# Four half tiles of K as a second seven-product unit, in a new order of the program, on one core

## The chip, the cores and the metric

The kernel runs on one core of one Trainium2 chip. The metric is the time of one execution in microseconds of device time. The runs of the kernel before gave a median of 203.47 us (three runs, 203.33 to 203.54).

## The reference

One input x of 2048 tokens by 640, normalized per token, feeds a linear attention (A) and a two-layer network with relu (B); the output joins them.

```python
def _A_ref(x, wqkv, wo):
    H = 32; Dh = D // H                      # D = 640
    q, k, v = ...                            # x @ wqkv, by heads
    phi = lambda t: jnp.where(t > 0, t + 1, jnp.exp(t)) + 1e-6
    pq, pk = phi(q), phi(k)
    kv = jnp.einsum("bhsd,bhse->bhde", pk, v)
    z = jnp.einsum("bhsd->bhd", pk)
    num = jnp.einsum("bhqd,bhde->bhqe", pq, kv)
    den = jnp.einsum("bhqd,bhd->bhq", pq, z)[..., None] + 1e-6
    return (num / den, heads joined) @ wo

def _B_ref(x, w1, w2):                       # w1: 640 x 1728, w2: 1728 x 640
    return jnp.maximum(x @ w1, 0) @ w2

xn = _layernorm(x)
return x + _A_ref(xn, wqkv, wo) * silu(_B_ref(xn, w1, w2))
```

All arrays are bf16.

## The kernel before

The 2048 tokens are 16 tiles of 128, in four chunks of 512. The kernel records its operations in a list and has two ways of ordering them. For TensorE (PE) and for SyncE (SP, which issues most DMAs) the order is that of `PROGRAM`, a string of some 500 words written out. For ScalarE (ACT), VectorE (DVE) and GpSimd (POOL) a planner, `Sched.place`, picks from the next 60 recorded operations by their costs (`cost`, an occupation and a duration in us for each form of instruction) and by due times counted back from PE's end. Both orders are fixed when the program is built; on the chip only semaphores hold an engine.

A head, not part of `PROGRAM`, loads x and weights, takes the statistics of the tiles, and computes K for tiles 0 to 7 (`K_mm`, L713) and the first blocks of h = xn @ w1 on the first chunk (`H_block`, L803). Then the words of `PROGRAM` follow:

- `n8` to `n15`: statistics (`bn`, L634; `aggr`, L638) and normalization (`LN_norm`, L653) of a tile, then its transpose by DMA on SP (`xnT_dma`, L702). `xa`, `xb`, `xc` load tiles 10 and 11, 12 and 13, 14 and 15; `wa` and `wb` load parts of w1.
- Units of seven products for eight. Four block products over two token blocks (or chunks) are formed with Strassen's sums: a unit has the steps s1, s5, s6, s2, s7, s3, s4, each a few matmuls into one of three PSUM banks, with two ScalarE copies (s1's and s5's results, L1209) and two VectorE additions (in s6 and s7) besides the evacuations. `a`, `b` are units of h over the first and second pair of chunks (512 columns), `p`, `q` those of Q, `m` a mixed one, `g` units of the product G = xn^T pk, `u` and `o` those of the second layer and of the output. They stand at L1202 (a, b, p, q, m, k) and L1029 (g, u, o).
- `k1` is a unit of K: tiles 9 and 13 (tile index 1 in the third and fourth chunk), with 320 columns a matmul. The sums of wk that it reads are made by `SK` (`k_S`). Its evacuations are exps and relus at L1331.
- `Ka8`, `Kb8` and so on compute one half (320 columns) of K for one tile by five matmuls, with an exp and a relu out of PSUM (`K_half`, L1486). Tiles 8, 10, 11, 12, 14 and 15 are done so. `K_fin` (L739) joins exp and relu to pk.
- `hh0` and `hh1` compute the last 64 columns of h for a pair of chunks (`H_half`, L821): twenty matmuls of 32 columns of weights, four of which stand side by side in the array (`tile_position`). Two ScalarE relus of 64 partitions each evacuate them (L827). `hh0` needs the transposed tiles 0 to 7, `hh1` tiles 8 to 15. `T1` forms sums of the transposed tiles for the `b`, `q` and `k` units.
- `y0` to `y15`, `zm`, `zs`, `zc`: POOL adds the tiles of pk into two sums by chained DMAs (L901); the column sum z comes of it. `dn` takes the denominators (L933) and four reciprocals (L946); `do0` to `do3` store them repeated into DRAM (L953), `rc0` to `rc3` read them back (L962), `dv` multiplies Q by them.
- `wv0`, `wv1` load w_v on ACT's queue (L544); `kv0`, `kv1` multiply G by it (L1599), `W0` to `W5` by wo (L1625), with small stores into the joined weight (L1640). `uT1` to `uT4` are sums of w2, `oT` sums of the joined weight.
- `e`, `f`, `l`: the last tiles of the output (L1834 and after).

The places of the units' rooms matter for `wv0`: g units copy a product into a part of wv_sb, so `wv0` waits until the g units have read it.

The change touches the words `Ka10`, `Kb10`, `Ka14`, `Kb14`, which become the unit `k2` (tiles 10 and 14), the places of `hh0` and `hh1` and of most other words, and the cost of an ACT operation. The whole unit is written already; its number is the tile index in the chunk:

```python
return unit(1, lambda half, k: wk[:, k, HN * half:HN * (half + 1)], ...,
            {1: ("kS", 1), 2: ("kS", 2), 4: ("kS", 4), 3: ("kS3",)}, out, out22, tile=i)
```

Of the kernel before, what the change touches and what calls it, by code (L numbers as in the profile page):

```python
# [32 lines left out]
def _cols(ap):  # L33
    n = 1
    for d in ap.shape[1:]:
        n *= d
    return n


def _wide(ap):  # L40
    return str(ap.dtype).endswith("float32")


def cost(E, fn):
    seen = _Seen()
    fn(seen)
    name, a, k = seen.call
    aps = [v for v in list(a) + list(k.values()) if hasattr(v, "shape") and hasattr(v, "dtype")]
    if E == "PE":
        if name == "transpose":  # L50
            return (0.107, 0.107) if a[1].offset % a[1].ap[0][0] < 640 else (0.056, 0.107)
        n = _cols(k["rhs"]) / 2400.0
        part = k["lhsT"].shape[-1] / 128.0 if k.get("tile_position") is not None else 1.0
        return max(n * part + 0.0025, 0.026), n
    n = max(_cols(v) for v in aps)
    if E == "ACT":
        more = 0.19 if k.get("accum_out") is not None else 0.0
        if n > 512:
            more += 0.02
        if n == 1 and k["func"] == ACTF.Silu:  # L60
            more += 1.3
        if hasattr(k.get("scale"), "shape"):
            more += 0.08
        if _wide(k["out"]) and _wide(k["in_"]) and k["out"].tensor.name == k["in_"].tensor.name:
            return 0.05 + 0.0009 * n, 0.17 + 0.00083 * n
        return 0.05 + 0.00083 * n + more, 0.17 + 0.00083 * n + more
    if E == "POOL":
        return (0.66, 0.66) if k.get("op") is ALU.pow else (0.33 + 0.0025 * n, 0.33 + 0.0025 * n) if n > 12 else (0.33, 0.33)
    out = k["out"] if "out" in k else a[0]
    wide = any(_wide(v) for v in aps if _cols(v) > 4)  # L70
    if name == "bn_stats":
        return 0.403, 0.478
    if n <= 12:
        return 0.13, 0.21
    if name == "reciprocal":
        return 0.815, 0.9
    if name in ("tensor_copy", "tensor_scalar", "memset"):
        more = 0.06 * sum(hasattr(k.get(q), "shape") for q in ("scalar1", "scalar2"))
        return (0.065 + 0.00105 * n, 0.15 + 0.00105 * n) if wide else (0.08 + 0.00024 * n + more, 0.16 + 0.00025 * n + more)
    if wide or name != "tensor_tensor":  # L80
        return 0.064 + 0.00105 * n, 0.155 + 0.00105 * n
    return 0.075 + 0.000515 * n, 0.148 + 0.00052 * n
# [12 lines left out]
class Sched:  # L95
# [44 lines left out]
    def _record(self, E, kind, fns, R, W, extra, sem=None):  # L140
# [5 lines left out]
        if kind == "dma":  # L146
            seen = _Seen()
            fns[0](seen)
            name, a, _k = seen.call
            o.turn = "transpose" in name  # L150
            o.occ = 1.3 if o.turn else 1.25 if E == "POOL" else 0.5
            fat = a[1].tensor.name
            if fat in ("in_A_wo_dram", "reg3") and E == "SP" and not o.turn:
                o.occ = 0.65
            size = 2.0
            for d in a[0].shape:
                size *= d
            names = [v.tensor.name for v in a[0:2]]
            o.byt = 0.6 if o.turn else size / {"scr": 205e3}.get(names[0], {"scr": 240e3}.get(names[1], 310e3))
            lag = 0.5 if names[1] == "scr" else 0.8 if names[1] == "reg3" and names[0] == "reg6" else 0.0  # L160
            if o.turn and names[0] == "wv_sb":
                o.byt = 2.0
            o.dur = 4.6 if E == "POOL" else 2.1 + o.byt if o.turn else 1.95 + o.byt + lag
        else:
            o.occ, o.dur = 0.0, 0.0
            o.turn = E == "PE" and any(_narrow(fn) for fn in fns)
            for fn in fns:
                occ, dur = cost(E, fn)
                o.dur = o.occ + dur
                o.occ += occ  # L170
# [1789 lines left out]
```

## Time and profile before

| | |
|---|---|
| median of three runs | 203.47 us (203.33 to 203.54) |
| the profiled execution's own time | 202.95 us |
| its span in the trace | 201.7 us |
| busy: PE, DVE, ACT, POOL | 198.4, 172.9, 129.1, 37.9 us |

The span is the time from the first to the last instruction of the profiled execution; the time around it is start and end of the launch. A busy PE is not PE at its peak: matmuls are pipelined and the trace models their ends, so lengths of work on PE are read from start to start, as the chain of waits does. In the page, PEld is the loading of weights, which runs beside PE. L12 is line 12 of the kernel before; in the changed kernel all lines behind the cost function are one higher.

### The profile page before, as it was taken

The numbers are of one execution on the slowest core, as the hardware profiler recorded it, in microseconds if no ns is written. First come the engines' busy times: TensorE is split into PE (matmuls) and PEld (weight loads), VectorE is DVE, ScalarE is ACT, GpSimd is POOL, SyncE is SP. The second block draws the span as 40 slices with busy tenths as digits, with TensorE's granted clock in tenths as the row PEclk, the third lists the DMA queues.
The fourth block names the chain that finished last, engine by engine and source line by source line (L and its number), as shares of the span: only waits on it lengthen the run. The fifth ranks groups of instructions, "written<-read, shape, count | busy, mean of one in ns | idle before, by whom it ended". The sixth has DMA issues, their size and how long they took to land.

```text
span 201.7 us, 3704 instructions
## 1 busy us (share of the span) xinstructions
PE 198.4 (98%) x1342; PEld 122.7 (61%) x1342; DVE 172.9 (86%) x411; ACT 129.1 (64%) x271; POOL 37.9 (19%) x66
## 2 busy tenths in 40 slices
PE   8999999999999999999999999999999999999995
PEld 7756544454554444445555677777767777777773
DVE  4998999999999987899975799789979799953566
ACT  5697969899889869998643213544445455452552
POOL 3183151253335550262200000000000000000000
DMA  6986992635556977365930988486983361020103
GB/s 204 330 218 112 268 237 48 165 95 118 126 117 137 183 154 183 65 132 88 240 65 0 313 246 194 150 216 182 368 293 79 128 184 68 26 81 28 65 33 98
DMA packets 38472, 30.43 MB, mean 151 GB/s; under 512 B 13750, under 2 KB 38454, under 8 KB 38454
## 3 DMA queue, kind: packets, MB, share of 16 engines
q1 hardware_dynamic: 32581, 23.28, 40.9%
q0 software_dynamic: 4624, 5.57, 14.4%
q10 hardware_dynamic: 1248, 1.35, 2.0%
q8 instruction: 10, 0.16, 0.4%
q14 instruction: 9, 0.07, 0.1%
HBM read 15.81 MB, written 5.24 MB: 104 GB/s over the span
## 4 chain that ended last, share of the span: by engine, by line
PE 96%; DMA 1%; DVE 1%; issue 0%; DVEq 0%
PE psT L1029 42%; PE psT L1202 30%; PE psT L713 9%; PE psT L803 5%; PE psT L1500 2%; DMA reg<-in_A_x_dram 1%; PE psT L1834 1%; PE psT L821 1%; PE psT L765 1%; PE psT L1625 1%; PE psT L686 1%; PE psT L1599 1%; PE psT L933 1%; DVE reg L974 0%; DVE stats L634 0%; DVE reg L679 0%
## 5 line engine op out<-in xcount | busy, mean ns | idle before, releaser
L1202 PE MATMUL psT<-reg 128*128 128x512 bf16 (+2 forms) x150 | 39.8, 374 | 0.0
L1029 PE MATMUL psT<-reg,regH 128*128 128x320 bf16 (+1 forms) x224 | 35.0, 299 | 0.0
L1029 PE MATMUL psT<-reg 128*128 128x320 bf16 (+1 forms) x178 | 29.2, 299 | 0.0
L1029 PEld LDWEIGHTS psT<-reg,regH 128*128 128x128 bf16 (+1 forms) x224 | 21.8, 98 | 8.6
L1202 PEld LDWEIGHTS psT<-reg 128*128 128x128 bf16 (+1 forms) x150 | 14.3, 98 | 16.8 <-DVE regH L974 0.8
L901 POOL DMA_DIRECT2D regH<-reg x16 | 18.4, 1210 | 30.1 <-DMA regH<-reg 11.7
L1036 ACT ACTIVATE reg<-psT 128x320 f32<-128x320 f32 (+1 forms) x24 | 10.4, 436 | 18.0 <-PE psT L1029 16.0
L1029 PEld LDWEIGHTS psT<-reg 128*128 128x128 f16 (+1 forms) x178 | 17.3, 98 | 7.4 <-issue 0.4
L974 DVE TENSOR_TENSOR reg<-reg 128x1024 f16<-128x1024 bf16 (+10 forms) x30 | 19.0, 649 | 0.1
L1661 ACT ACTIVATE wv_sb<-psT 128x320 bf16<-128x320 f32 (+1 forms) x23 | 9.6, 423 | 14.0 <-PE psT L1029 13.7
L1252 ACT ACTIVATE regH<-psT 128x512 bf16<-128x512 f32 (+1 forms) x24 | 15.0, 631 | 4.1 <-PE psT L1202 3.9
L974 DVE TENSOR_TENSOR psT<-psT,reg 128x320 f32<-128x320 f32 (+1 forms) x21 | 11.4, 545 | 5.4 <-PE psT L1029 5.1
L713 PE MATMUL psT<-reg 128*128 128x320 bf16 x100 | 15.5, 299 | 0.0
L1029 PE MATMUL psT<-reg,pqT 128*128 128x320 bf16 (+1 forms) x84 | 15.3, 299 | 0.0
L634 DVE BATCH_NORM_STATS2 stats<-reg 128x6 f32<-128x320 bf16 x32 | 14.0, 474 | 1.3 <-DMA reg<-in_A_x_dram 1.3
L974 DVE TENSOR_TENSOR reg<-psT,reg 128x320 bf16<-128x320 f32 (+2 forms) x17 | 8.5, 502 | 5.9 <-PE psT L1029 5.9
L713 PEld LDWEIGHTS psT<-reg 128*128 128x128 bf16 x100 | 9.8, 98 | 5.6
L1036 ACT ACTIVATE psT<-psT 128x320 f32<-128x320 f32 x17 | 7.0, 423 | 7.4 <-PE psT L1029 7.4
L780 ACT ACTIVATE regE<-psT 128x512 bf16<-128x512 f32 x16 | 9.9, 617 | 2.9 <-PE psT L1202 1.9
L1486 ACT ACTIVATE regE<-psT 128x320 bf16<-128x320 f32 x24 | 10.5, 514 | 0.6 <-PE psT L713 0.6
L1849 ACT ACTIVATE reg<-psT 128x640 bf16<-128x640 f32 (+1 forms) x14 | 7.4, 569 | 4.5 <-PE psT L1029 4.5
L642 POOL TENSOR_TENSOR rsy<-rsv,mhalf 128x1 f32<-128x1 f32 x16 | 10.1, 635 | 1.1
(169 smaller groups left out, 395.6 us busy)
## 6 DMA issues: line engine op xcount, KB each, us to landing
regH<-reg POOLq DMA_DIRECT2D x16, 320.0 KB, 3.7
reg<-in_B_w_dram SPq DMA_DIRECT2D x12, 320.0 KB, 5.0
scr<-rden SPq DMA_DIRECT2D x4, 640.0 KB, 6.2
reg<-in_A_x_dram SPq DMA_DIRECT2D x4, 640.0 KB, 8.0
out_dram<-reg SPq DMA_DIRECT2D x14, 160.0 KB, 1.9
regE<-scr SPq DMA_DIRECT2D x3, 640.0 KB, 4.9
reg<-in_A_x_dram SPq DMA_DIRECT2D x4, 320.0 KB, 3.5
reg<-in_A_wo_dram SPq DMA_DIRECT2D x6, 160.0 KB, 5.0
```

The lines of the kernel that those rows point to most:

```text
L634: sc.op("DVE", lambda eng: eng.bn_stats(stats[:, t, a, :], xv[:, HN * a:HN * (a + 1)]), R=[("xin", xs(t))], W=[("stats", t, a)])
L642: sc.op("POOL", lambda eng: eng.tensor_tensor(out=rsy[:, t:t + 1], in0=rsv[:, t:t + 1], in1=mhalf[:, :], op=ALU.pow), R=[("rsv", t), ("mha ...
L713: fns.append(lambda eng, a=a, k=k, lhs=lhs: eng.matmul(ps[bk[a]][:, 0:HN], lhsT=lhs, rhs=wk[:, k, HN * a:HN * (a + 1)], start=(k == 0), st ...
L780: exps.append(sc.op("ACT", lambda eng: eng.activation(out=e_, in_=src, func=ACTF.Exp), R=[key], W=[("er_e", es)]))
L803: sc.group("PE", [(lambda eng, k=k: eng.matmul(ps[b], lhsT=w1_col(k, P * f, P), rhs=src[:, k, :], start=(k == 0), stop=(k == C - 1))) for ...
L901: dma("POOL", lambda eng: eng.dma_start(zacc[a], src, **kw), R=[key] + after, W=[("zacc", a)], chain=zchain[a])
L974: sc.op("DVE", lambda eng: eng.tensor_tensor(out=out, in0=in0, in1=in1, op=op), R=R, W=W, extra=extra)
L1029: sc.group("PE", [(lambda eng, k=k, lhs=lhs, rhs=rhs: eng.matmul(ps[b][:, 0:HN], lhsT=lhs, rhs=rhs, start=(start and k == 0), stop=(k == n ...
L1036: sc.op("ACT", lambda eng: eng.activation(out=dst, in_=ps[b][:, 0:HN], func=ACTF.Copy), R=[("ps", b)], W=[dkey], extra=extra)
L1202: sc.group("PE", [(lambda eng, k=k, lhs=lhs, rhs=rhs: eng.matmul(ps[b][:, 0:nn], lhsT=lhs if tile is None else rhs, rhs=rhs if tile is Non ...
L1252: sc.op("ACT", lambda eng: eng.activation(out=dst, in_=ps[b], func=ACTF.Relu), R=[("ps", b)], W=[("hT", j, f)], extra=ex)
L1486: sc.op("ACT", lambda eng, func=func, slot=slot: eng.activation(out=ek[:, eks(t), slot, HN * a:HN * (a + 1)], in_=ps[b][:, 0:HN], func=fun ...
```

## The change

1. The four groups `Ka10`, `Kb10`, `Ka14` and `Kb14` of `K_half` are taken out, and the unit `k2` stands in `PROGRAM`.
2. `hh0` and `hh1` stand one behind the other; before, `hh0` came early and `hh1` 34 us later. Most other words have other places, too: among PE's words the units and K halves are mixed in another way, and on SP `xb` and `xc` come behind tile 8's transpose, tiles 9 to 15 are transposed in one run, `rc0` and `rc1` come earlier, `do3` comes before `do1`, and the stores of the W words come behind `rc1`.
3. In the planner's costs an ACT operation whose output has fewer than 128 partitions occupies ACT 0.14 us longer.

The operations of all other words are the same. The diff, with the program cut to the stretches that the text speaks of:

```diff
         if hasattr(k.get("scale"), "shape"):
             more += 0.08
+        turn = 0.14 if k["out"].shape[0] < 128 else 0.0
         if _wide(k["out"]) and _wide(k["in_"]) and k["out"].tensor.name == k["in_"].tensor.name:
             return 0.05 + 0.0009 * n, 0.17 + 0.00083 * n
-        return 0.05 + 0.00083 * n + more, 0.17 + 0.00083 * n + more
+        return 0.05 + 0.00083 * n + more + turn, 0.17 + 0.00083 * n + more
...
 PROGRAM = """
-H111 H14 H15 xb H112 T0 H110 Q14 a0.s1 a0.s5 xa SQ n8 hh0 a0.s6 Q04 ... p1.s3 xc wa p1.s7 wb a1.s2 n11 a1.s6 Ka8 n13 SH1 p1.s4 SK a1.s3 n10 n15 p0.s5 mv6 n14 a1.s7 n9 p0.s1 ...
-  ... a1.s4 p0.s6 a2.s5 a2.s1 ... Kb14 a3.s5 a3.s1 b0.s4 Ka15 a3.s6 hh1 b1.s1 a3.s7 ... Kb10 SM ... Ka14 ... Ka10 GS0 ...
-  ... g0.s3 uSa0 g1.s1 GS1 w2c GT4 g0.s7 wo g1.s5 do0 g1.s6 g0.s4 uT3 wv0 g1.s7 g1.s2 uT1 g1.s3 uT2 wv1 g1.s4 u0.s1 kv1 do1 kv0 W5 rc0 ...
+H110 H112 H14 H111 T0 H15 SQ SK xa Q14 a0.s1 a0.s5 Q04 a0.s6 p1.s5 p1.s1 n8 wa xb a0.s2 a0.s7 p1.s6 rb ... wb p1.s7 p1.s2 a1.s6 xc n9 SH1 p1.s4 a1.s2 Kb8 a1.s7 n12 n11 p0.s1 n10 n13 ... n14 a1.s4 n15 ...
+  ... a2.s3 a2.s7 hh0 hh1 T1 a2.s4 b0.s1 b0.s5 Ka11 b0.s6 k1.s1 k1.s5 ... k1.s3 k1.s4 Kb15 q0.s1 q0.s5 b1.s1 q0.s6 ... k2.s5 k2.s1 b1.s4 a3.s5 y3 k2.s6 Kb11 y9 a3.s1 k2.s2 k2.s7 k2.s3 a3.s6 k2.s4 a3.s2 ...
+  ... g1.s1 GS1 g1.s5 g1.s6 g0.s7 g0.s2 w2c g1.s7 g1.s3 wv0 ZS uT3 wo do0 g1.s2 g1.s4 g0.s4 wv1 sl rc0 ... do3 do1 u0.s1 u0.s5 kv1 u0.s6 rc1 kv0 W5 ...
 """
```

More of the change, by code (lines that the diff above doesn't have):

```diff
@@ L344 @@
 PROGRAM = """
-H111 H14 H15 xb H112 T0 H110 Q14 a0.s1 a0.s5 xa SQ n8 hh0 a0.s6 Q04 p1.s1 a0.s3 Kb8 rb a0.s7 p1.s5 a0.s2 p1.s6 a0.s4 p1.s2 a1.s5 a1.s1 n12 p1.s3 xc wa p1.s7 wb a1.s2 n11 a1.s6 Ka8 n13 SH1 p1.s4 SK a1.s3 n10 n15 p0.s5 mv6 n14 a1.s7 n9 p0.s1 Kb12 Ka12 a1.s4 p0.s6 a2.s5 a2.s1 p0.s2 p0.s3 a2.s6 p0.s7 a2.s2 T1 a2.s7 p0.s4 a2.s3 a2.s4 Kb11 b0.s1 k1.s1 k1.s5 Ka11 k1.s6 b0.s5 k1.s2 b0.s6 k1.s7 b0.s2 k1.s3 b0.s7 k1.s4 b0.s3 Kb14 a3.s5 a3.s1 b0.s4 Ka15 a3.s6 hh1 b1.s1 a3.s7 b1.s5 a3.s3 b1.s6 a3.s2 a3.s4 y8 b1.s2 q0.s5 q0.s1 b1.s7 Kb15 y12 y11 q0.s6 b1.s3 y7 b1.s4 q0.s2 ZS q0.s7 q0.s3 q1.s1 y9 y4 y3 y6 q0.s4 y1 q1.s5 q1.s6 b2.s5 Kb10 SM y5 b2.s1 q1.s2 y13 q1.s3 b2.s6 q1.s7 Ka14 y2 y0 y14 b2.s7 y15 q1.s4 b2.s3 b2.s2 b2.s4 b3.s1 Ka10 GS0 GT1 GT2 b3.s5 w2a m1.s1 b3.s6 m1.s5 b3.s2 m1.s6 b3.s3 SH2 GT3 m1.s2 zm m1.s7 b3.s7 m1.s3 m1.s4 y10 zs b3.s4 c0 b4.s1 b5.s5 w2b b5.s1 w2d b4.s5 b4.s6 b4.s2 c1 b4.s7 b4.s3 b5.s6 b4.s4 g0.s5 g0.s1 b5.s3 b5.s2 b5.s7 zc g0.s6 b5.s4 g0.s2 dn g0.s3 uSa0 g1.s1 GS1 w2c GT4 g0.s7 wo g1.s5 do0 g1.s6 g0.s4 uT3 wv0 g1.s7 g1.s2 uT1 g1.s3 uT2 wv1 g1.s4 u0.s1 kv1 do1 kv0 W5 rc0 sl u0.s5 W2 uSb0 W4 u0.s6 do2 uT4 u0.s2 W3 u0.s7 u0.s3 u2.s1 uSa2 W1 dv0 u2.s5 u0.s4 u2.s6 W0 uSa1 u2.s2 uSb2 rc1 u1.s1 uSa4 u1.s5 xre u1.s6 u1.s2 u2.s7 uSb1 u2.s3 oS0 uSb4 u1.s7 u1.s3 u2.s4 u1.s4 oT o0.s5 u4.s5 o0.s1 u4.s1 o0.s6 do3 o0.s2 u4.s6 o0.s3 o0.s7 rc2 u4.s7 o0.s4 uSa3 u4.s3 o1.s1 u4.s2 oS1 o1.s5 dv1 o1.s6 u4.s4 o1.s2 o1.s7 o2.s1 oS2 o2.s5 o1.s3 o1.s4 o2.s6 o2.s2 u3.s5 o2.s7 u3.s1 rc3 o2.s3 uSa6 uSb3 o2.s4 u3.s6 uSa5 o3.s1 oS3 u3.s2 o3.s5 o3.s6 u3.s7 dv2 u3.s3 oS4 o3.s7 o3.s2 u3.s4 u5.s5 u5.s1 uSb5 o3.s3 o3.s4 u5.s6 o4.s1 o4.s5 u5.s2 uSb6 o4.s6 u5.s7 u5.s3 oS5 o4.s2 o4.s7 u5.s4 o4.s3 o4.s4 u6.s1 o5.s1 o5.s5 u6.s5 uSa7 u6.s6 o5.s6 o5.s2 u6.s2 o5.s7 u6.s3 dv3 u6.s7 o5.s3 o5.s4 u6.s4 u7.s1 oS6 o6.s1 u7.s5 o6.s5 u7.s6 o6.s2 o6.s6 u7.s2 o6.s3 o6.s7 uSb7 e1 u7.s7 o6.s4 e0 u7.s3 e3 f0 u7.s4 f1 f3 l0 l1
@@ new lines @@
+H110 H112 H14 H111 T0 H15 SQ SK xa Q14 a0.s1 a0.s5 Q04 a0.s6 p1.s5 p1.s1 n8 wa xb a0.s2 a0.s7 p1.s6 rb a0.s3 a0.s4 p1.s3 a1.s5 a1.s1 wb p1.s7 p1.s2 a1.s6 xc n9 SH1 p1.s4 a1.s2 Kb8 a1.s7 n12 n11 p0.s1 n10 n13 a1.s3 p0.s5 Ka8 p0.s6 n14 a1.s4 n15 y7 p0.s2 a2.s5 a2.s1 p0.s7 Ka12 a2.s6 Kb12 p0.s3 a2.s2 p0.s4 y8 a2.s3 a2.s7 hh0 hh1 T1 a2.s4 b0.s1 b0.s5 Ka11 b0.s6 k1.s1 k1.s5 b0.s2 k1.s6 b0.s7 b0.s3 k1.s7 k1.s2 b0.s4 k1.s3 k1.s4 Kb15 q0.s1 q0.s5 b1.s1 q0.s6 b1.s5 q0.s2 b1.s6 q0.s7 y6 q0.s3 b1.s3 q0.s4 mv6 b1.s7 b1.s2 y2 k2.s5 k2.s1 b1.s4 a3.s5 y3 k2.s6 Kb11 y9 a3.s1 k2.s2 k2.s7 k2.s3 a3.s6 k2.s4 a3.s2 a3.s7 a3.s3 q1.s1 q1.s5 a3.s4 q1.s6 b2.s5 q1.s2 SM y12 b2.s1 y13 Ka15 y0 q1.s7 w2a b2.s6 y4 y1 y14 GT1 GT2 y5 y15 q1.s3 y11 q1.s4 b2.s7 zm b2.s3 GS0 GT3 b2.s2 b3.s1 b2.s4 b3.s5 SH2 y10 b3.s6 m1.s5 m1.s1 b3.s2 b3.s7 m1.s6 b3.s3 m1.s2 b3.s4 m1.s7 zs b4.s5 GT4 m1.s3 b4.s1 m1.s4 c1 b4.s6 b5.s5 b5.s1 w2d c0 b4.s7 b4.s2 b4.s3 b5.s6 b4.s4 g0.s5 w2b g0.s1 b5.s7 b5.s3 b5.s2 zc g0.s6 b5.s4 dn g0.s3 g1.s1 GS1 g1.s5 g1.s6 g0.s7 g0.s2 w2c g1.s7 g1.s3 wv0 ZS uT3 wo do0 g1.s2 g1.s4 g0.s4 wv1 sl rc0 uSa0 uSb0 uT2 uT1 do3 do1 u0.s1 u0.s5 kv1 u0.s6 rc1 kv0 W5 u0.s7 u0.s2 W4 uT4 uSa2 dv1 u0.s3 W2 u0.s4 W1 W3 W0 xre dv0 uSa1 u1.s1 oT uSb2 uSb1 u1.s5 u2.s1 u2.s5 u1.s6 u2.s6 u2.s2 uSa4 u2.s7 oS0 u1.s7 u1.s3 u2.s3 u1.s2 u2.s4 u1.s4 do2 o0.s5 o0.s1 u4.s5 o0.s6 u4.s1 o0.s2 o0.s3 uSb4 o0.s7 u4.s6 o0.s4 u4.s2 o1.s1 oS2 uSa6 u4.s7 oS1 o1.s5 o1.s2 o1.s6 uSa3 u4.s3 o1.s3 o1.s7 u4.s4 o1.s4 u3.s5 o2.s1 u3.s1 rc3 o2.s5 o2.s2 o2.s6 u3.s6 uSb3 o2.s7 dv3 o2.s3 uSa5 u3.s7 o2.s4 u3.s2 o3.s1 rc2 u3.s3 u3.s4 oS3 uSb6 dv2 o3.s2 o3.s5 oS4 o3.s6 u5.s1 u5.s5 o3.s7 o3.s3 uSb5 u5.s6 u5.s2 o3.s4 u5.s7 u5.s3 o4.s1 u5.s4 o4.s5 o4.s2 o4.s6 u6.s1 u6.s5 oS5 u6.s6 o4.s3 o4.s7 u6.s7 o4.s4 u6.s3 oS6 o6.s1 o6.s5 u6.s2 o6.s6 u6.s4 o6.s2 o6.s7 o6.s3 e3 uSa7 o6.s4 u7.s1 o5.s5 o5.s1 u7.s5 o5.s6 u7.s6 o5.s7 o5.s2 o5.s3 u7.s2 o5.s4 e0 f0 uSb7 u7.s7 u7.s3 f3 e1 u7.s4 f1 l0 l1
```

## The prediction

> **What bounds the kernel now.** I read the page first, then the waits by engine, the chain that ended last, and the grouped rows. The page gives the span, and busy time by engine.
>
> ```profile
> span 201.7 us, 3704 instructions
> PE 198.4 (98%) x1342; PEld 122.7 (61%) x1342; DVE 172.9 (86%) x411; ACT 129.1 (64%) x271; POOL 37.9 (19%) x66
> ```
>
> The list of PE's waits holds one row, at the start:
>
> ```profile
> PE psT L602 <- PEq L1945: 0.8, 1, 0.8
> ```
>
> The chain in order of time (start, length, what) runs over matmuls without a break to the last product:
>
> ```profile
> 22.78 5.40 PE psT L803 x25
> ...
> 30.12 1.19 PE psT L821 x20
> ...
> 34.01 0.68 PE psT L713 x5
> 34.69 6.69 PE psT L1202 x31
> ...
> 198.64 0.36 PE psT L1834 x5
> ```
>
> So 25 matmuls of 512 columns take 5.40 us, 0.216 each, and five of 320 columns 0.68, 0.136 each. The time is the sum of PE's work behind a head that ends at 22.78 and a tail behind L1834; the change leaves both alone. An edit is worth what it takes out of PE's queue, less what it makes PE wait. ScalarE and VectorE do not set the end, but have little room where the change works (windows: busy PE, PEld, DVE, ACT, POOL, then the granted clock, 1.00):
>
> ```profile
> 40.00:60.00 20.00, 20.00 (x109) 10.39 (x108) 19.62 (x53) 18.27 (x41) 8.15 (x14) 1.00 0.55 120
> 60.00:80.00 20.00, 20.00 (x117) 9.50 (x115) 17.95 (x47) 17.52 (x39) 9.31 (x8) 1.00 0.79 166
> ```
>
> **The second unit.** Ka10, Kb10, Ka14 and Kb14 are four groups of five L713 matmuls, 20 in all. The unit k2 has products of 2, 3, 3, 3, 2, 2, 2 and 1 matmuls of the same 320 columns: 18. Off PE: 2 x 0.136 = 0.27 us. The exps and relus stay at eight. Added are two ScalarE copies out of PSUM and two VectorE additions, for which these are the nearest rows (grouped by form: count, busy, mean ns):
>
> ```profile
> L1209 ACT ACTIVATE psT<-psT 128x320 f32<-128x320 f32 x1 | 0.5, 500 | 0.0
> L974 DVE TENSOR_TENSOR psT<-psT,wv_sb 128x320 f32<-128x320 f32 x2 | 1.0, 498 | 0.2 <-PE psT L1029 0.2
> ```
>
> That is 1.0 us more for each engine between 60 and 80 us, where ACT is busy 17.5 and DVE 17.95 of 20. The idle 2 us hide it; without that cover it costs up to 1.0. The sums of weights that k2 reads are already made for k1.
>
> **The half chunks together.** In the changed order both L821 groups follow each other, 40 in a run. The timeline around hh1:
>
> ```profile
> 63.70 0.60 PE L1202 MATMUL psT<-regX,rden 128*128 128x512 f16 x2
> 64.24 1.26 PE L821 MATMUL psT<-reg 128*32 128x512 bf16 x20
> 65.43 0.60 PE L1202 MATMUL psT<-reg 128*128 128x512 bf16 x2
> 65.55 1.21 ACT L827 ACTIVATE regH<-psT 64x512 bf16<-64x512 f32 x2
> 66.61 0.42 DVE L974 TENSOR_TENSOR regH<-regH,wv_sb 128x512 f16<-128x512 bf16 x1
> 66.79 0.58 ACT L1209 ACTIVATE psT<-psT 128x512 f32<-128x512 f32 x1
> 66.94 0.69 DVE L974 TENSOR_TENSOR regH<-psT,wv_sb 128x512 bf16<-128x512 f32 x1
> ```
>
> The L1202 pair ahead occupies PE until 63.70 + 2 x 0.216 = 64.13. Twenty narrow matmuls, four side by side, are five passes: 1.08 us. The next full product starts at 65.43, 1.30 after 64.13, so 0.22 goes into turning the array to narrow and back. One run instead of two saves one such pair: 0.22 us.
>
> **The cost function.** `turn` is no instruction; it changes only the order that the planner writes for ScalarE and VectorE. The row fits it: from the first half evacuation (65.55) to the next copy (66.79) are 1.24 us, about 0.61 for each half.
>
> **Old and new waits of PE on ScalarE.** A start later than the matmuls ahead allow tells where an evacuation came late. The largest behind the head:
>
> ```profile
> 46.92 0.75 ACT L1252 ACTIVATE regH<-psT 128x512 f16<-128x512 f32 x1
> 47.14 0.59 PE L1202 MATMUL psT<-regE 128*128 128x512 f16 x2
> 47.72 1.04 PE L1202 MATMUL psT<-reg 128*128 128x512 bf16 x4
> ```
>
> PE was free at 47.14 + 0.43 = 47.57 and started at 47.72, behind an evacuation that ended at 47.67: 0.15 lost, at a2.s1. In the new order a2.s1 has other neighbours, and this goes. New ones come. From 22.78 the new order has 122 matmuls of 512 and 20 of 320 columns ahead of hh0, so hh0 starts at 22.78 + 26.3 + 2.7 + 0.1 = 51.9, hh1 at 53.0, the products behind it at 54.2, and b0.s6, behind 7 x 0.216 + 0.68, at 56.4. It needs the copy of b0.s1. ScalarE can begin with hh0's first half 1.31 after the block's start (65.55 - 64.24), at 53.25; three halves of 0.61 and one evacuation of 0.6 stand ahead of the copy, which then ends at 53.25 + 1.83 + 0.6 + 0.6 = 56.3. The margin is 0.1, and full evacuations run from 0.58 to 0.75 in the rows above: 0 to 0.25 lost. The same size, by likeness only, at q0.s6, whose copy stands behind the exps and relus of k1. I take 0.1 for each, 0.2 together; the ends are 0 and 0.5.
>
> **What comes closer behind DMAs.** First the transposes. hh1 needs tile 15's, and SP issues those of tiles 9 to 15 in one run (a row of the timeline; then the line's own duration and landing; then the groups of VectorE's work ahead of tile 9):
>
> ```profile
> 44.68 6.59 SPq L702 DMA_TRANSPOSE reg<-reg  x5
> ...
> L702 SPq DMA_TRANSPOSE reg<-reg x16: 1200/1276/1966, 13.4 to 50.0; - x16
> ...
> DMA to landing us min/median/max: 2.6/2.6/5.3
> ...
> L634 DVE BATCH_NORM_STATS2 stats<-reg 128x6 f32<-128x320 bf16 x32 | 14.0, 474 | 1.3 <-DMA reg<-in_A_x_dram 1.3
> L653 DVE TENSOR_SCALAR reg<-reg,mv,rsy 128x640 bf16<-128x640 bf16 x16 | 6.5, 424 | 0.5 <-POOL rsy L642 0.5
> L638 DVE BATCH_NORM_AGGREGATE mv<-stats 128x2 f32<-128x12 f32 x16 | 3.0, 199 | 0.3
> L974 DVE TENSOR_TENSOR psT<-psT,wv_sb 128x512 f32<-128x512 f32 x10 | 7.0, 699 | 1.0 <-PE psT L1202 0.9
> ```
>
> One goes every (6.59 - 1.28)/4 = 1.33 us. By the same count of matmuls PE is through with a1.s6 at 38.75, and its result is to be had 0.2 later; VectorE then does its addition (0.70), four bn_stats (4 x 0.47), two aggregates (2 x 0.2) and tile 9's normalization (0.42): at 42.4, or some 0.5 earlier, since neighbours overlap by about 0.09 (66.61 + 0.42 against 66.94). Six more issues: 49.9 to 50.4; landed 52.5 to 53.0. hh1 is due at 53.0: margin 0 to 0.5. I take nothing lost.
>
> Second, wv0 on ScalarE's queue, which PE needs for kv1. It waits for g1.s7's addition, and VectorE now does two weight sums (uT1, uT3) right ahead of that:
>
> ```profile
> L974 DVE TENSOR_TENSOR reg<-reg 128x2240 f16<-128x2240 bf16 x2 | 2.5, 1316 | 0.0
> ...
> L946 DVE RECIPROCAL rden<-regE 128x128 bf16<-128x128 f32 x4 | 3.6, 933 | 0.0
> ...
> reg<-in_B_w_dram SPq DMA_DIRECT2D x12, 320.0 KB, 5.0
> scr<-rden SPq DMA_DIRECT2D x4, 640.0 KB, 6.2
> ...
> reg<-in_A_x_dram SPq DMA_DIRECT2D x4, 320.0 KB, 3.5
> ...
> wv_sb<-in_A_wqkv_dram ACTq DMA_DIRECT2D x1, 480.0 KB, 4.8
> ...
> wv_sb<-in_A_wqkv_dram ACTq DMA_DIRECT2D x1, 320.0 KB, 4.2
> ```
>
> Let T be when PE is through with g1.s7. g0.s7 stands 16 matmuls ahead, so its addition can start at T - 2.0; it (0.5), two sums of 1.32 and g1.s7's addition (0.5) bring the issue to T + 1.6, or T + 2.4 with a reciprocal of 0.93 just begun. At 4.2 us wv0 lands at T + 5.8 to T + 6.6. PE has 46 matmuls of 320 columns before kv1: due at T + 6.26, from 0.45 behind the landing to 0.35 ahead of it. I take nothing lost, the middle.
>
> On SP the read rc1 now stands ahead of the small W stores, and oT waits for those; the products of u2 and u1 stand between on PE and hide it. On POOL the chained additions into z end with tile 10's as before, with G's last products and two h units between it and PE's use. Both at nothing.
>
> The sum: -0.27 - 0.22 - 0.15 + 0.2 = -0.44. The profiled run took 202.95, its span 201.7 and 1.25 around it; it becomes 202.5. The median of the runs shown, 203.47, is 0.5 above the profiled one; the same step gives 203.0. What a measurement here can tell from no change is about 0.2%, 0.41 us, so this is faster by hardly more than the bound, at 203.06.
>
> **The rivals.** *Evacuations eat the gain.* ScalarE has four halves in a row at the half chunks and two more copies at k2. If four tight places cost the 0.15 of a2.s1 each, the new waits are 0.6 for 0.2, and the time is 203.4. For: the small margin at b0.s6. Against: in before both engines are as full from 40 to 60, and PE's list of waits is empty there. Chance 0.18, within 0.2%.
>
> *wv0 late.* Loads beside others took 4.8 and 5.0 in the rows above, against 4.2. Then it is up to 1.1 late, and the time 203.1 to 204.1. For: do0's 640 KB are in flight on SP's queue. Against: the last reciprocal, which do0 waits for, stands ahead of g0.s7's addition, so do0 is issued 3.6 us before wv0, over half of its 6.2. Chance 0.12, of it 0.03 slower. The Trainium skill, "DMA: Bandwidth & Descriptors", Queues, rings and completion order, says that each DMA engine takes turns between queue rows packet by packet, and that SP and ACT own one row each. By it wv0 moves at half its rate as long as do0 lasts and no longer; the 4.8 of the larger load agrees, no run here shows it for wv0.
>
> *The other side: transposes late at hh1.* Tile 9 stands behind tile 12's statistics on VectorE, and the load of tiles 12 and 13 is issued behind tile 8's transpose and a weight load. a0.s6 is done at 22.78 + 41 x 0.216 = 31.6; its addition and tile 8's normalization end at 32.9, the transpose's issue at 34.2, so the load goes at about 34.7. At 3.5 us it lands at 38.2, at 5.0 at 39.7; VectorE wants it at 39.65. At 6.5 all seven transposes slide by 1.5, PE stands at hh1 with everything queued behind it, and the time is 203.0 + 1.0 to 1.5, 204.0 to 204.5. It decides from a landing of about 6 us, a slide of 0.9 over the margin. Chance 0.10, of it 0.08 slower and the rest within.
>
> *It does not do what it says*: the turns return elsewhere, or the two matmuls were hidden: 203.5. Against it, PE's rows leave no cover. Chance 0.03.
>
> **The numbers.** Forecast 0.57, faster by over 0.2%, from 202.6 to 203.06. Same 0.18 + 0.09 + 0.02 + 0.03 = 0.32; slower 0.11. The range runs from 202.6 (no new wait, and other small gaps gone) to 203.7, which leaves out the upper half of wv0's case and the transposes'.
>
> **What would show it.** Right: 18 K matmuls for 20, one run of 40 L821 of about 2.3 us in the chain, no row among PE's waits but the first, and the last L1834 0.4 to 0.6 earlier. Wrong: PE behind a transpose at hh1 or behind wv0 at kv1, or gaps of PE behind ScalarE's copies that come to over 0.3.

## The result and the profile after

The changed kernel took 202.73 us (median of seven runs, 202.49 to 202.89), the kernel before 203.33 beside it (203.16 to 203.54): a ratio of 0.9969, with a 95% interval of 0.9957 to 0.998. That is 0.60 us, or 0.3%, faster. The forecast was 0.44 us of gain, as 203.0 with a range of 202.6 to 203.7.

The page of the changed kernel, the list of PE's waits, and rows of its chain of waits (start, length, what):

```profile
span 201.4 us, 3693 instructions
...
PE 197.8 (98%) x1340; PEld 122.6 (61%) x1340; DVE 175.1 (87%) x413; ACT 130.9 (65%) x273; POOL 37.9 (19%) x66
```
```profile
PE psT L603 <- PEq L1946: 0.8, 1, 0.8
PE psT L714 <- DMA reg<-in_A_wqkv_dram: 0.3, 1, 0.3
```
```profile
23.09 5.40 PE psT L804 x25
...
52.14 2.27 PE psT L822 x40
...
198.33 0.36 PE psT L1835 x5
```

Two matmuls are gone (1340 for 1342), two operations each were added on ScalarE and VectorE, and the half chunks are one run of 40 narrow matmuls of 2.27 us. The profiled run took 202.65 us, its span 201.4. The second wait is new, but it lies in the head, which the change leaves alone: `PROGRAM` begins at 23.09 here and at 22.78 in the kernel before. The last product ends at 198.69 for 199.00, 0.31 earlier where 0.4 to 0.6 had been forecast, since the head took 0.31 longer in this execution. From the start of `PROGRAM` to its last product that makes 175.60 us for 176.22, 0.62 less. The chain books a group from the end of the one before it, 0.07 to 0.16 us behind its first start in the timeline; by starts the length is 175.86 for 176.48, again 0.62 less. This length is what the rest of the text compares, by starts, since the head differs from one execution to the next. What PE loses at a step is likewise read by starts: the step's start, less the start of the matmul ahead of it and the time that this one needs (0.216 us for 512 columns).

The stretch from the half chunks on, in the timeline (start, length, engine, line, operation):

```profile
50.03 1.28 SPq L703 DMA_TRANSPOSE reg<-reg  x1
...
52.07 2.34 PE L822 MATMUL psT<-reg 128*32 128x512 bf16 x40
53.39 1.82 ACT L828 ACTIVATE regH<-psT 64x512 f16<-64x512 f32 x3
54.35 0.60 PE L1203 MATMUL psT<-regE,reg 128*128 128x512 f16 x2
55.21 0.60 ACT L1253 ACTIVATE regH<-psT 128x512 f16<-128x512 f32 x1
55.70 0.59 ACT L1210 ACTIVATE psT<-psT 128x512 f32<-128x512 f32 x1
56.22 0.59 ACT L1210 ACTIVATE reg<-psT 128x512 f32<-128x512 f32 x1
56.55 0.59 PE L1203 MATMUL psT<-reg,pqT 128*128 128x512 f16 x2
56.83 0.59 ACT L828 ACTIVATE regH<-psT 64x512 bf16<-64x512 f32 x1
...
63.39 0.64 ACT L1210 ACTIVATE psT<-psT 128x512 f32<-128x512 f32 x1
63.56 0.59 PE L1203 MATMUL psT<-reg 128*128 128x512 bf16 x2
64.08 1.04 PE L1203 MATMUL psT<-reg,pqT 128*128 128x512 f16 x4
```

The narrow run begins at 52.07 and the next product at 54.35: 2.28 for ten passes of 0.216, so 0.12 for the way back, and 0.09 stands ahead of the run. b0.s6 starts at 56.55, 0.26 behind the end of its copy (55.70 + 0.59). The one place where PE stands behind ScalarE is q0.s6: the pair ahead is through at 63.56 + 0.43 = 63.99, the copy ends at 64.03, and the product starts at 64.08, 0.09 late and 0.05 to 0.06 behind the copy. In the traces here no product starts less than 0.05 to 0.06 behind the evacuation that it waits for. Taking this as the floor, 0.2 of the 0.26 at b0.s6 are spare.

### The profile page after: what moved, and what is told of

Same layout as the page of the kernel before. It is cut to its first block, busy times and chain, and to the rows that moved or that the text cites. A ratio compares the mean times of both kernels' runs of the same rounds, so it can differ in the third digit from the quotient of the medians.

```text
span 201.4 us, 3693 instructions
## 1 busy us (share of the span) xinstructions
PE 197.8 (98%) x1340; PEld 122.6 (61%) x1340; DVE 175.1 (87%) x413; ACT 130.9 (65%) x273; POOL 37.9 (19%) x66
## 4 chain that ended last, share of the span: by engine, by line
PE 95%; DMA 3%; SPq 1%; DVE 0%; issue 0%; DVEq 0%
PE psT L1030 43%; PE psT L1203 31%; PE psT L714 8%; PE psT L804 5%; DMA reg<-in_A_wqkv_dram 3%; PE psT L1501 2%; PE psT L1835 1%; PE psT L822 1%; PE psT L766 1%; PE psT L1626 1%; PE psT L1600 1%; PE psT L934 1%; DVE reg L975 0%; SPq L564 0%; SPq L540 0%
## 5 line engine op out<-in xcount | busy, mean ns | idle before, releaser
L1203 PE MATMUL psT<-reg 128*128 128x512 bf16 (+2 forms) x159 | 41.7, 370 | 0.0
L1203 PEld LDWEIGHTS psT<-reg 128*128 128x128 bf16 (+1 forms) x159 | 15.5, 98 | 16.1 <-DVE reg L975 0.7
L975 DVE TENSOR_TENSOR psT<-psT,reg 128x320 f32<-128x320 f32 (+1 forms) x22 | 11.9, 542 | 5.6 <-PE psT L1030 5.1
L1030 PE MATMUL psT<-reg,pqT 128*128 128x320 bf16 (+1 forms) x84 | 16.3, 299 | 0.0
L1850 ACT ACTIVATE reg<-psT 128x640 bf16<-128x640 f32 (+1 forms) x14 | 8.0, 570 | 9.2 <-PE psT L1030 9.2
L714 PE MATMUL psT<-reg 128*128 128x320 bf16 x80 | 12.3, 299 | 0.0
L975 DVE TENSOR_TENSOR reg<-psT,reg 128x320 f32<-128x320 f32 (+2 forms) x19 | 9.5, 504 | 1.4 <-PE psT L1030 1.3
L714 PEld LDWEIGHTS psT<-reg 128*128 128x128 bf16 x80 | 7.8, 98 | 4.3 <-ACT regH L808 0.3
L1030 PEld LDWEIGHTS psT<-reg,pqT 128*128 128x128 bf16 (+1 forms) x84 | 8.2, 98 | 3.2
```

Source lines behind the costliest of these rows:

```text
L714: fns.append(lambda eng, a=a, k=k, lhs=lhs: eng.matmul(ps[bk[a]][:, 0:HN], lhsT=lhs, rhs=wk[:, k, HN * a:HN * (a + 1)], start=(k == 0), st ...
L975: sc.op("DVE", lambda eng: eng.tensor_tensor(out=out, in0=in0, in1=in1, op=op), R=R, W=W, extra=extra)
L1030: sc.group("PE", [(lambda eng, k=k, lhs=lhs, rhs=rhs: eng.matmul(ps[b][:, 0:HN], lhsT=lhs, rhs=rhs, start=(start and k == 0), stop=(k == n ...
L1203: sc.group("PE", [(lambda eng, k=k, lhs=lhs, rhs=rhs: eng.matmul(ps[b][:, 0:nn], lhsT=lhs if tile is None else rhs, rhs=rhs if tile is Non ...
```

## The experiments

Where a run's time spread hid the effect, the trace decides. Below, the **lag** of a step is the time from `PROGRAM`'s first matmul to the step's first, less the same in the changed kernel. So b0.s6 starts 56.55 - 22.93 = 33.62 us after `PROGRAM`'s first matmul starts there. Each lag is read from one trace of each kernel. In the kernels t4 to t9 the order of ScalarE, VectorE and GpSimd is held by a list, so that an edit moves nothing else; in t1 to t3 the planner makes it anew for the edited program.

### The second unit taken back

```diff
-... y2 k2.s5 k2.s1 b1.s4 a3.s5 y3 k2.s6 Kb11 y9 a3.s1 k2.s2 k2.s7 k2.s3 a3.s6 k2.s4 a3.s2 ...
+... y2 Ka10 b1.s4 a3.s5 y3 Kb11 y9 a3.s1 Kb10 Ka14 a3.s6 Kb14 a3.s2 ...
```

> The changed kernel, but the second unit is taken back: tiles 10 and 14 go through Ka10, Kb10, Ka14 and Kb14, put where k2.s1, k2.s2, k2.s3 and k2.s4 stood; all else stays. Theory (the unit is worth its two matmuls): PE gets 20 matmuls of 320 columns for 18, 2 x 0.136 = +0.27 us over the changed kernel, so 203.0 for 202.73, and 1342 matmuls on the page. Rival (the unit's copies and additions on ScalarE and VectorE cost as much as it saves, and the gain comes from the rest): within 0.1 us of the changed kernel. A second rival (the unit's seven short steps also separate other steps from their evacuations): over 0.5 us slower, with new gaps of PE behind ScalarE or VectorE.

The median was 203.24 (203.11 for the kernel before in the same runs, ratio 0.9999, 0.9976 to 1.0023); runs spread over 1.2 us. The lag is nothing up to the unit, 0.27 at a3.s2, right behind the last half, and 0.37 from a3.s7 to the end. The 0.27 are the two matmuls to the digit. The other 0.10 is a wait at a3.s7 for VectorE's addition of a3.s6, in VectorE's order as planned anew:

```profile
75.50 0.69 DVE L975 TENSOR_TENSOR psT<-psT,wv_sb 128x512 f32<-128x512 f32 x1
75.52 0.81 PE L1203 MATMUL psT<-reg 128*128 128x512 bf16 x3
...
76.25 0.60 PE L1203 MATMUL psT<-regX,reg 128*128 128x512 f16 x2
```

The three matmuls are through at 75.52 + 0.65 = 76.17, the addition ends at 76.19, and PE goes on at 76.25. So the unit's own term was right, and its copies and additions cost nothing here; the rival that sets them against the gain falls.

### The planner's cost put back

```diff
-        turn = 0.14 if k["out"].shape[0] < 128 else 0.0
+        turn = 0.0
```

> The changed kernel with the planner's cost of a half-partition evacuation put back (turn = 0.0); PE's order and SP's stay as they are, and only the order in which ScalarE and VectorE take their work can differ. Theory (the edit is no instruction; it makes the planner's clock right by 0.14 us per half, which can keep one evacuation from being queued too early): 0 to +0.2 us over the changed kernel, seen as a gap of PE behind a ScalarE copy between 52 and 65 us. Rival (the edit carries the result): over 0.4 us slower, at the time of the kernel before, 203.3 or more. Second rival (no change of order matters): within 0.05 us.

The median was 203.07 (ratio 0.9996, 0.9974 to 1.0018). The lag is nothing up to hh1 and 0.45 from b0.s6 on, 0.46 at the end. The timeline shows the place:

```profile
53.21 2.44 ACT L828 ACTIVATE regH<-psT 64x512 f16<-64x512 f32 x4
...
55.68 0.60 ACT L1253 ACTIVATE regH<-psT 128x512 f16<-128x512 f32 x1
56.17 0.59 ACT L1210 ACTIVATE psT<-psT 128x512 f32<-128x512 f32 x1
...
56.82 0.60 PE L1203 MATMUL psT<-reg,pqT 128*128 128x512 f16 x2 [0.28 <-ACT psT L1210]
```
Without the 0.14 the planner takes all four halves in a row; with it, the fourth goes behind the copies of b0.s1 and b0.s5. One half is 2.44 / 4 = 0.61 us of ScalarE, and less the 0.2 spare at b0.s6 that leaves 0.4, for 0.45 measured. I had expected 0 to 0.2: the cost alone, not the order, was in my mind. The rival was right in substance: without a line that adds no instruction, 0.45 of the 0.62 us are lost again. This is not one more term beside the turn and the two matmuls. The line keeps them from being eaten by a wait. The kernel before with this line alone was not run; planned with it, where the two half chunks stand apart, ScalarE's order stays as it was and one pair of VectorE's operations changes places.

### The half chunks together in the kernel before

```diff
-... SQ n8 hh0 a0.s6 ... a3.s6 hh1 b1.s1 ...
+... SQ n8 a0.s6 ... a3.s6 hh0 hh1 b1.s1 ...
```

> The kernel before with one word moved: hh0 goes from the front of the order to the place right ahead of hh1, nothing else. Theory (a turn pair of the array is worth 0.22 us, but hh0 was also the cover of a0.s6, which started 0.84 us after VectorE's sum for it was ready, of which some 0.06 is the floor, with hh0's 1.19 us ahead of it): PE stands 0.4 us or more at a0.s6, and again behind the four half evacuations in a row at b1, so the time is 0.2 to 1.5 us above the kernel before, 203.5 to 204.8. Rival (the two half chunks together are worth their turn wherever they stand): 0.2 us below the kernel before, 203.1. In both, the chain should show one run of 40 narrow matmuls of 2.3 us.

205.55 us, 1.0122 times the kernel before (1.0083 to 1.0161): 2.4 us slower, more than I had expected. The run of 40 is there, and so is the turn that it saves:

```profile
66.35 2.34 PE L821 MATMUL psT<-reg 128*32 128x512 bf16 x40
67.67 2.44 ACT L827 ACTIVATE regH<-psT 64x512 f16<-64x512 f32 x4 [0.71 <-PE psT L821]
...
70.16 0.60 PE L1202 MATMUL psT<-reg,pqT 128*128 128x512 f16 x2 [0.28 <-ACT regH L827]
```
```profile
PE psT L713 <- DMA reg<-in_A_wqkv_dram: 1.1, 1, 1.1
...
PE psT L1202 <- DVE regE L974: 0.7, 1, 0.7
PE psT L1202 <- ACT regE L1486: 0.5, 1, 0.5
PE psT L1202 <- ACT regH L827: 0.3, 1, 0.3
```

The losses are at several places. The list counts idle time from the modelled end of the matmul before, so each row is 0.1 to 0.2 short of the loss by starts (0.89 at a0.s5, 0.69 at p1.s5, 0.45 at b1.s5). By the list p1.s5 stands 0.5 behind a relu of K, a0.s5 0.7 behind one of VectorE's sums, and b1.s5 0.3 behind the last of the four halves (67.67 + 2.44 = 70.11), whose bank it writes. At a0.s6, the place that I had named, hh0's 1.3 us are gone from the path, and yet a0.s6 starts no earlier after `PROGRAM`'s first matmul than in the kernel before: the cover was spent in full, most of it one step earlier, at a0.s5. This profiled run took 206.75, 1.2 above the median, and its head was 1.0 late (the wait for a load of wk, 1.1); part of the wait at a0.s5 belongs to that, as the last experiment shows, and how much of the 2.4 does is not settled. What is settled is the sign: the two stretches side by side, without a new order around them, lose some ten times what the turn gives.

### One transpose more on SP's queue

```diff
     def xnT_dma(t):
+        if t == 9:
+            dma("SP", ... eng.dma_start_transpose(place of tile 15, xn[:, 9, :]), R=[("xn", 9)], W=[("xnT", 15)])
```

> The changed kernel with one more DMA transpose on SP's queue, right ahead of tile 9's (it reads tile 9's rows and writes the place of tile 15, which tile 15's own transpose overwrites); the order of every engine is held as it is in the changed kernel. Theory (tiles 9 to 15 go out back to back, one per 1.32 us, and tile 15 lands 0.50 us ahead of hh1): PE stands 1.32 - 0.50 = 0.82 us at hh1, all behind it slides by that, less what the later small gaps give back (0.1), so +0.7 to +0.8 us over the changed kernel, 203.5, and the list of PE's waits gets a row at L822 behind a DMA. Rival (the transposes are paced by the normalizations on VectorE, not by their own queue): the extra one falls into idle time of the queue and the time stays within 0.1 us of the changed kernel.

203.41 us (203.11 for the kernel before in the same runs; ratio 1.0022, 0.9997 to 1.0047). The lag is 0.21 at Ka12, 0.67 at hh1, 0.75 at q0.s6, 0.82 at b1.s3 and 0.97 from q0.s4 to the end. Chain and waits:

```profile
50.87 2.63 DMA reg<-reg
53.50 0.04 issue
53.54 1.26 PE psT L826 x20
```
```profile
PE psT L826 <- DMA reg<-reg: 0.3, 1, 0.3
```

PE stands at hh1 until tile 15's transpose has landed at 53.50, and did so before, at Ka12, for tile 12's. So the queue of transposes sets the pace, and the rival that the normalizations do falls. The sum at hh1 was less than the 0.82 that I had worked out, since tile 15 landed 1.13 later and not 1.32: the run of transposes began 0.27 earlier after `PROGRAM`'s start than in the changed kernel. What I had not seen is that it does not end there: q0.s6 loses 0.07 more behind its copy than in the changed kernel, and b1.s3 and q0.s4 stand behind VectorE's additions for another 0.2. Why VectorE is late there was not followed further.

### Nine turns of the array

```diff
-... a2.s7 hh0 hh1 T1 ...
+... a2.s7 d0 d1 d2 d3 d4 d5 d6 d7 d8 hp0 hp1 ... hp9 T1 ...        (t5)
+... a2.s7 hp0 d0 hp1 d1 hp2 d2 ... hp8 d8 hp9 T1 ...               (t6)
```

`hp0` to `hp9` are the ten passes of hh0 and hh1, `d0` to `d8` the nine full matmuls.

> The changed kernel with nine extra full-array matmuls of 128 columns, all in a block ahead of hh0, into a bank that nothing reads; the passes of the half chunks follow each other as before, and the order of every engine is held. It is the control of the next run. Both theories: nine matmuls at 0.216 x 128/512 = 0.054 us, +0.49 us over the changed kernel from the first product of the order to the last; hh1's margin to the transposes grows by as much and b0.s6's stays.

> The same nine extra matmuls, but one between each two of the ten narrow passes of the half chunks, so the array turns to narrow and back ten times and not once. Theory (each turn to narrow and back costs PE 0.21 us, as the change saved by going from two pairs to one): nine pairs more than in the control, 9 x 0.21 = +1.9 us over it, +2.4 over the changed kernel, with the 40 narrow matmuls spread over some 4.6 us. Rival (the 0.21 was the loss of one particular place, such as the matmul with fresh weights behind the run): +0.2 or less over the control. Second rival (only the way in costs, 0.09 us): +0.8.

The control took 203.19 us (ratio 0.9994, 0.9978 to 1.001), its length is 176.36, 0.50 over the changed kernel's; the other took 205.03 (1.0072, 1.0046 to 1.0097). First the control's chain, then that of the kernel with the full matmuls between:

```profile
51.80 0.50 PE psT L1547 x9
52.30 2.27 PE psT L833 x40
```
```profile
52.15 0.33 PE psT L833 x4
52.48 0.16 PE psT L1547
...
56.58 0.33 PE psT L833 x4
```

A pass and a full matmul take 0.33 + 0.16 = 0.49 us where they need 0.216 + 0.054 = 0.27: 0.22 for each turn to narrow and back. From the first narrow matmul to b0.s1 it is 2.93 us in the control (52.23 to 55.16) and 5.42 in the other (52.08 to 57.50): 2.49 more, of which nine matmuls are 0.50, as the control shows, and nine turns 1.99, against 1.9 expected. The price belongs to the turn and to no particular place. Nor is it a matter of fresh weights: in the control the nine full matmuls, each with a load of weights of its own, follow each other at 0.055 us. The Trainium skill, "TensorEngine Tiling (Array Packing)", Key Properties, says that a change of the tiling mode, not of the tile alone, drains TensorE. The trace agrees: passes of four different tiles follow each other at 0.216 us, and only a change to the full array and back costs the 0.22.

### One copy more on ScalarE

```diff
+            sc.group("ACT", [copy of ps[ba] into a free bank, copy of ps[ba] into ps[bb]], ...)      # b0.s1
```

> The changed kernel with one more ScalarE copy of 128x512 right ahead of the copy of b0.s1 (into a free bank of PSUM that nothing reads); the order of every engine is held. Theory (ScalarE has no room here: b0.s6 started 0.26 us after that copy's end, of which 0.06 is the floor, so 0.2 are spare, and q0.s6 already stands 0.09 behind a copy): 0.50 to 0.59 for the copy less 0.2 spare, +0.3 to +0.4 us at b0.s6, and up to 0.15 more at q0.s6; +0.3 to +0.55 over the changed kernel. Rival (ScalarE is 65% busy and off the path): within 0.05 us of the changed kernel.

203.29 us (ratio 0.9992, 0.9978 to 1.0005). The lag is 0.28 at b0.s6, 0.30 at q0.s6 and 0.33 at the end.

```profile
55.83 1.08 ACT psT L1210 x2
56.91 0.05 issue
56.96 1.15 PE psT L1203 x6
```

The second copy makes 1.08 of the 0.59, so 0.49 more, of which 0.2 were spare. The chain of waits, which ran over PE alone, now runs over ScalarE. An engine that is busy 65% of the span is on the path here.

### The changed kernel again, and q0.s6 moved

```diff
-... q0.s1 q0.s5 b1.s1 q0.s6 b1.s5 q0.s2 ...
+... q0.s1 q0.s5 b1.s1 b1.s5 q0.s6 q0.s2 ...        (t9)
```

> The changed kernel once more, with the order of every engine written out as a list (the same instructions in the same order). All theories: from the first product of the order to the last the same length as in its first profile, 175.86 us, within 0.05, if only the head differs from one execution to the next; and 0.5 to 0.7 us below the kernel before in the median.

> The changed kernel with one pair of PE's steps exchanged: b1.s5 goes ahead of q0.s6, so that q0.s6 comes 2 x 0.216 us later; the order of ScalarE, VectorE and GpSimd is held. Theory (q0.s6 stands 0.09 us behind the copy of q0.s1; b1.s5 has 0.9 us to spare): the gap at q0.s6 goes and none takes its place, so 0.09 us less between the first product and the last, 175.77 for 175.86; the median can't tell that. Rival (the wait only moves, since q0.s6's addition on VectorE comes 0.43 later and q0.s7, q0.s4 and b1.s6 stand behind it; q0.s4 started 0.15 behind VectorE): no gain, or up to 0.3 slower, with a gap at q0.s7 or q0.s4.

The same instructions once more took 202.77 us against 203.31 for the kernel before (ratio 0.9969, 0.9951 to 0.9987), which confirms the result. But the length of `PROGRAM` was 176.32 in that profile for 175.86, not the same. The lag arises in the first 9 us: 0.13 at a0.s1, 0.42 at a0.s5, 0.45 at a0.s6, and from there to the end it stays between 0.45 and 0.46. The timeline of that run, then of the changed kernel:

```profile
23.56 4.42 SPq L703 DMA_TRANSPOSE reg<-reg  x2
...
29.43 0.69 DVE L975 TENSOR_TENSOR regE<-reg 128x1024 f16<-128x1024 bf16 x1 [0.75 <-DMA reg<-reg]
29.45 0.60 PE L1203 MATMUL psT<-reg 128*128 128x512 bf16 x2
30.17 0.60 PE L1203 MATMUL psT<-regE,pqT 128*128 128x512 f16 x2
```
```profile
24.07 2.69 SPq L703 DMA_TRANSPOSE reg<-reg  x2
```

The issue of the head's last transpose ended 1.2 us later (23.56 + 4.42 against 24.07 + 2.69), VectorE and a0.s1 waited for it, and a0.s5 for VectorE's sum. So 0.46 us hang on a DMA of the head. The lags of the other experiments were read step by step for that reason, and begin behind a0.s6. Two other kernels lost time at the same steps in their traces: the one with the full matmuls between had 0.56 by a0.s6, which is why its stretch is measured from the first narrow matmul, and the half chunks together in the kernel before (t3) lost 0.23 at a0.s1. The 0.62 of the result does not hang on it: in neither of those two traces does PE lose over 0.04 us at a step up to a0.s6, but for the turn at hh0.

With q0.s6 moved the median was 202.58 us (ratio 0.9976, 0.9958 to 0.9995), and the length 175.78, 0.08 less than the changed kernel. The lag is -0.10 from q0.s2 on: the wait is gone. 0.02 of it comes back at q0.s4, which now starts 0.06 behind VectorE's addition of q0.s7, the floor. So it is the best of the kernels by its trace; the medians cannot tell 0.08 us.

## Why the prediction was right

The sign, the mechanism and the size of both main terms hold.

- *Two matmuls fewer, -0.27*: measured 0.27 by taking the unit back. Its copies and additions hide, as assumed, and the halves in its place add a wait of 0.10 in that plan, which I had not counted.
- *One turn fewer, -0.22*: 0.22 by the nine extra turns.
- *The old wait at a2.s1, -0.15*: it is gone. So is a smaller one, 0.05 at b2.s6, that I had left out; b2.s6 started at 80.67 there, 0.05 behind its copy (79.99 + 0.63).
- *The new waits, +0.2*: measured 0.09. This is the term that was mis-sized. Read as times in the trace, the reckoning to b0.s6 looks nearly exact: hh0 forecast for 51.9, the copy's end for 56.3, b0.s6 due at 56.4; measured 52.07, 56.29 and 56.55. But that is luck in part, as `PROGRAM` began 0.3 later than in the profile of before, which moves all three alike. Counted from hh0's start, b0.s6 came 4.48 later for 4.5 forecast, and the copy ended 4.22 later for 4.34 (1.31 + 1.83 + 0.6 + 0.6). The evacuation ahead of the copy was the error: I had given it 0.6, and it held ScalarE for 0.49 (55.21 to 55.70), since the copy starts before it has ended. So the margin was 0.26 and not 0.1, and nothing was lost where I had taken 0.1. At q0.s6, taken at 0.1 by likeness only, it was 0.09; that this size came out is luck.
- *The sum*: -0.27 - 0.22 - 0.15 - 0.05 + 0.09 = -0.60, for 0.62 between the two traces and 0.60 between the medians. The last 0.02 are spread over losses too small to name. The forecast's 0.44 differs from the 0.60 by the 0.11 too many for new waits and the 0.05 of b2.s6. That 203.0 is 0.27 above the measured 202.73 comes half from there and half from the kernel before, whose median was 203.33 beside the changed one and 203.47 when I started from it.
- *The cost function*: I wrote that it changes only the order, and left its worth open. It is 0.45 us, and the row that I quoted for it, 0.61 us for a half, was the price: one half more ahead of b0.s1's copy. My reckoning to b0.s6 had three halves ahead of that copy, the order that the line makes, so its worth was in the sum without being named; with the line left out, the new waits would have been 0.54 for 0.09.
- *Transposes at hh1*: margin forecast 0 to 0.5; tile 15 was issued at 50.03, landed at 52.67 and hh1 started at 53.16, 0.50 later. The rival by the load of tiles 12 and 13 cost PE nothing, but it began: the load was issued at 35.88 for 34.7, 0.9 later when counted from `PROGRAM`'s start, and VectorE stood 0.16 us behind it:

```profile
39.97 1.28 DVE L635 BATCH_NORM_STATS2 stats<-reg 128x6 f32<-128x320 bf16 x3 [0.16 <-DMA reg<-in_A_x_dram]
```

The margin at hh1 covered those 0.16. What a slide beyond it costs, the extra transpose shows: PE stood there, and `PROGRAM` became 0.97 longer, near the 1.0 that I gave for the rival's milder case.
- *wv0 at kv1*: it was not late. Rows of the changed kernel (DMA issues with KB and us to landing; timeline):

```profile
wv_sb<-in_A_wqkv_dram ACTq DMA_DIRECT2D x1, 320.0 KB, 3.0
```
```profile
116.73 0.66 SPq L954 DMA_DIRECT2D scr<-rden  x1
119.94 0.38 ACTq L545 DMA_DIRECT2D wv_sb<-in_A_wqkv_dram  x1
124.58 0.81 PE L1600 MATMUL psT<-reg,wv_sb 128*128 128x120 bf16 x15
```

PE was through with g1.s7 at 118.33, so the issue at 119.94 came 1.6 later, the early end of the forecast's 1.6 to 2.4. It landed at 122.96, 1.6 ahead of kv1, where I had forecast from 0.35 late to 0.45 early: the load took 3.0 us, not 4.2. do0's store was issued 3.2 us ahead of it. The packets by queue (by their sizes q1 is SP's and q10 ScalarE's: packets, MB, share of the 16 DMA engines' time) show how far the two met, from 121.05 to 123.00:

```profile
q10 hardware_dynamic: 272, 0.33, 59.8%
q1 hardware_dynamic: 48, 0.03, 7.6%
```

Of do0's 640 KB only 0.03 MB were left when the packets of wv0 began to move. So the rule of taking turns that I weighed, of the Trainium skill's "DMA: Bandwidth & Descriptors", Queues, rings and completion order, is neither borne out nor refuted by it. I had also read the 4.8 of the larger load of before as agreeing with that rule. Its packets do not say so. From 112.8 to 113.9, when most of it moved in the kernel before, it had the engines nearly alone:

```profile
q10 hardware_dynamic: 312, 0.40, 97.0%
q1 hardware_dynamic: 43, 0.03, 9.3%
```

SP had issued three loads of w_o by 112.4, which landed from 116.06 on, but whether their packets were ready in this stretch is not shown, so this does not refute the rule either.

## What to carry to other kernels

When one engine is busy 98% of the span, an edit is worth what it takes out of that engine's queue, and here two small terms, added up from the rows, came out within 0.05 us; but each of them holds only with an order around it that keeps the evacuations ahead. A planner's cost that is wrong by 0.14 us for one kind of instruction can put one instruction too many ahead of the one that the full engine waits for, and that cost nearly as much as the two edits bring together (0.45 us for 0.49); when an edit brings slow instructions together, check the planner's figure for them first. Where differences are below the scatter of whole runs, compare the traces step by step from a common start: the step at which the lag jumps names the wait.

## What was not expected of the hardware

Two executions of the same instructions agreed to 0.01 us over 167 us of PE's work, from a0.s6 to the last product, and differed by 0.45 in the 9 us before, where a transpose of the head was issued 1.2 us later. The scatter of this kernel's time (203.48 to 202.25 for the same kernel) has one source there, which the traces of t3 and t6 show as well; whether it is the only one was not tried.
